# First bucket pass of a graph kernel: chunks in one stated order, equal source buckets counted on GpSimd

## The chip, the cores and the metric

The kernel runs on one core of a Trainium2 chip. Its engines have queues of their own and run side by side: TensorE (PE; its weight loads are listed as PEld), VectorE (DVE), ScalarE (ACT), GpSimd (POOL) and SyncE (SP), which here only issues transfers. The metric is the device time of one execution in microseconds (us), lower is better; the time given is the median of the runs.

## The reference

A graph of 10,000 nodes has 160,000 random edges (src, dst). Node features x (10,000 x 128) are passed along the edges seven times with a symmetric norm, and a small transformer block then reads the eight feature vectors of each node:

```
h = x; toks = [x]
for _ in range(7):
    msg = h[src] * deg_inv_sqrt[src, None] * deg_inv_sqrt[dst, None]
    h = segment_sum(msg, dst, N)
    toks.append(h)
tok = stack(toks, axis=1)                  # (N, 8, 128)
# layernorm, one attention block over the 8 tokens with wq, wk, wv, wo,
# then a softmax-weighted readout over the tokens with w_r -> (N, 128)
```

## The kernel before

The edges are sorted on the chip first, so that the seven hops can be done as products with 0/1 matrices. Destinations are cut into 79 buckets of 128 nodes, sources likewise into 72 buckets and a few cells. The change concerns the first bucket pass, which sorts the edges by destination bucket, and what stands around it. An edge sits at one of 128 partitions and 1250 columns; 50 columns make a chunk, 25 chunks in all.

**Preparing** (`pass_a`, lines 293 to 318). src and dst are loaded, and integer steps on DVE make `key` (the destination bucket), `d1` (src >> 3, plus 1) and `d2` (the other bits of src with the position of dst in its bucket). `first_rows` loads x on ACT's queue and scales its 79 tiles of 128 rows there. `lag` compares each column with the earlier ones of its chunk (49 comparisons on DVE, summed by PE into `wl`).

**The chunks** (lines 319 to 387). For each chunk: `oh` compares the keys with all 79 buckets (DVE, L226); `U` counts over the partitions (50 matmuls, L329), and ACT copies it to `U2`; `ux` multiplies it with `oh` (DVE, L239); `R` adds these up (17 matmuls, L243 and L244); `rk` reduces this to the rank of each edge in its bucket (DVE, L247). From the rank come one-hot rows over the 128 slots: `rv` for nine pairs of columns on DVE (L373) and `rs` for the other sixteen on ACT, one instruction per column (L360). `o` are the products of `oh` with `d1` and with `d2` (six instructions on DVE, L232). 50 matmuls (L385) add up `ta`, slot by bucket, in two halves, and `take` sums the halves on DVE into `TT` (L333), which then holds the packed edge of each slot. A scheduler sets the order of the instructions here from a loop that is already staggered: ranks of the next chunk and counts of the one after stand between the products of this one.

**The first table** (`first_table`, called at chunk 2). DVE takes the largest scaled entry of x (`mc`, L205), a few small steps make a power of two from it, and four times ACT writes 20 tiles as f16 (L177) while DVE writes what the rounding left (L178). Four transfers on SP's queue store the table.

**Decoding** (`decode`, lines 389 to 412). Once all of `TT` is there, nine passes over 128 x 2000 words get the source bucket `kB` and the 16-bit pattern `word` out of it on DVE and ACT; `lag_rows` compares `kB` with its earlier chunks (24 comparisons on DVE) and PE adds these up to `wB` (L285), the number of equal buckets ahead of each slot.

Then comes the second pass, interleaved with the first hop in an order written out by hand (`FRONT`), for which `pb_open` makes some constants. It reads `kB`, `wB`, `word` and `TT`. Six more hops and the attention follow. In the attention and the hops GpSimd has products (L1261, L1367), a scaling (L846) and a small copy (L737), and DVE small products (L1304, L1339) and a scaled subtraction (L838), by which the prediction prices and judges GpSimd's work.

Of the kernel before, what the change touches and what calls it, by code (L numbers as in the profile page):

```python
# [24 lines left out]
CELL = 334  # L25
CNODES = 196
# [32 lines left out]
2S1.2 0X1 3V1 1w0.2 2g2 3d1 3K3  # L59
"""  # L60


class Hops:
# [123 lines left out]
    def first_rows(self):  # L187
        nc, A = self.nc, self.nc.scalar
        tab0 = self.tab[0]
        y = self.tab[1].bitcast(F32)  # L190
        nc.gpsimd.memset(y[:, NT - 1:, :], 0.0)
        nc.gpsimd.memset(tab0[:, NT:, :], 0.0)
        h = NT // 2
        for a, b in ((0, h), (h, NT - 1)):
            nc.scalar.dma_start(y[:, a:b, :], self.x[a * 128:b * 128, :].rearrange("(t p) d -> p t d", p=128))
        nc.scalar.dma_start(y[:N - (NT - 1) * 128, NT - 1, :], self.x[(NT - 1) * 128:, :])
        for t in range(NT):
            A.activation(y[:, t, :], y[:, t, :], AF.Copy, scale=self.disT[:, t:t + 1])

    def first_table(self):  # L200
        nc, V = self.nc, self.nc.vector
        tab0, y = self.tab[0], self.tab[1].bitcast(F32)
        with self.tc.tile_pool(name="ft", bufs=1) as sp, self.tc.tile_pool(name="ftp", bufs=1, space=PSUM) as pp:
            mc = sp.tile([128, 1], F32, name="mc")
            V.tensor_reduce(mc, y[:, :NT, :], axis=mybir.AxisListType.XY, op=ALU.max, apply_absolute_value=True)  # L205
# [12 lines left out]
            q = self.pow2(pp, sp, m2, 2.0 ** 8)
            V.tensor_mul(self.sinv, self.sinv, q[:, 1:2])
            V.tensor_copy(self.q2, q[:, 0:1])  # L220


    def onehot(self, pool, name, key, n, size=None, **kw):
# [3 lines left out]
                                     self.io2[:, None, :n, :].to_broadcast([128, m, n, 2]), op=ALU.is_equal)  # L227
# [5 lines left out]

    def rank(self, wp, wu, R, oh, U2, w):

        nc, T = self.nc, self.nc.tensor
        m, nk, k = oh.shape[1], oh.shape[2], 5
        ux = wu.tile([128, m, nk, 2], F16, name="ux", tag="ux")
        nc.vector.tensor_tensor(ux, oh, U2[:, None].to_broadcast([128, m, nk, 2]), op=ALU.mult)  # L239
        R = R[:, :m * k * 2].rearrange("p (j k i) -> p j k i", k=k, i=2)  # L240
        for s in range(0, nk, k):
            e = min(k, nk - s)
            T.matmul(R[:, :, :e, :], self.id16, ux[:, :, s:s + e, :], start=s == 0, stop=False, skip_group_check=True)  # L243
        T.matmul(R[:, :, 0, :], self.id16, w, start=False, stop=True, skip_group_check=True)  # L244
        rk = wp.tile([128, m, 2], F16, name="rk")
        with nc.allow_low_precision("whole numbers; those over 2048 only have to stay large"):
            nc.vector.tensor_reduce(rk, R.rearrange("p j k i -> p j i k"), axis=X, op=ALU.add)  # L247
        return rk
# [21 lines left out]
    def lag_rows(self, ep, pp, key, w, m):  # L270

        V, T, k = self.nc.vector, self.nc.tensor, key.shape[2]
        n = 512 // k * k
        W = pp.tile([128, -(-m * k // n), 512], F32, name="W")
        flat = lambda z: z.rearrange("p m k -> p (m k)")
        parts = [(b, b * n, min(m * k, b * n + n)) for b in range(W.shape[1])]
        for b, r, e in parts:
            T.matmul(W[:, b, :e - r], self.id16, self.zero16[:, :e - r], start=True, stop=False, skip_group_check=True)
        for l in range(1, m):
            eq = ep.tile(list(key.shape), F16, name="eq")  # L280
            V.tensor_tensor(eq[:, l:], key[:, l:], key[:, :m - l], op=ALU.is_equal)
            for b, r, e in parts:
                r1 = max(r, l * k)
                if r1 < e:
                    T.matmul(W[:, b, r1 - r:e - r], self.id16, flat(eq)[:, r1:e], start=False, stop=(l + 1) * k >= e,  # L285
                             skip_group_check=True)
        for b, r, e in parts:
            self.nc.scalar.copy(flat(w)[:, r:e], W[:, b, :e - r])

    def pass_a(self):  # L290
        tc, nc, V, A, T, G = self.tc, self.nc, self.nc.vector, self.nc.scalar, self.nc.tensor, self.nc.gpsimd
        with ExitStack() as c:
# [5 lines left out]
            with tc.tile_pool(name="pe", bufs=1) as ep, tc.tile_pool(name="peq", bufs=3) as eqp, \  # L298
# [5 lines left out]
                it = ep.tile([128, 3, NCOL], I32, name="it")  # L304
                V.tensor_single_scalar(it[:, 0], ed[:, 1, :, 0], 7, op=ALU.arith_shift_right)
# [4 lines left out]
                V.tensor_tensor(it[:, 2], it[:, 2], it[:, 0], op=ALU.bitwise_or)  # L310
# [12 lines left out]

            def count(ch):
                oh = self.onehot(wp, "oh", K4[:, ch], NK)
                U = pp.tile([128, NK], F32, name="U")
                for j in range(NP):
                    for i in range(2):
                        T.matmul(U, self.tri, oh[:, j, :, i], start=j + i == 0, stop=j + i == NP)  # L329
                return oh, U  # L330

            def take(ch, ta):
                V.tensor_reduce(self.TT[:, ch, :NK], ta.rearrange("p h k -> p k h"), axis=X, op=ALU.add)  # L333

            def ranks(ch, oh, U):
                U2 = wp.tile([128, NK, 2], F16, name="U2")
                A.activation(U2, U[:, :, None].to_broadcast([128, NK, 2]), AF.Copy)
# [3 lines left out]
                A.activation(rb, rk[:, VP:], AF.Copy, scale=-2.0 ** 21, bias=16.0)
# [4 lines left out]
            cuts = (0, VP), (VP, VL), (VL, NP)
            ta = None
            for ch in range(NCH):
                if ch == 2:
                    self.first_table()  # L350
                oh, rk, rb = st
                ros = [wp.tile([128, b - a, 2, 128], F8, name=f"rs{a}") for a, b in cuts[1:]]
                for (a, b), ro in zip(cuts[1:], ros):
                    if ch == NCH - 1 and b == VL:
                        V.tensor_tensor(ro, rk[:, a:b, :, None].to_broadcast([128, b - a, 2, 128]),
                                        self.iof[:, None, None, :].to_broadcast([128, b - a, 2, 128]), op=ALU.is_equal, saturate=False)
                        continue
                    for j in range(a, b):
                        for i in range(2):
                            A.activation(ro[:, j - a, i, :], self.iof, AF.Abs_reciprocal_sqrt, scale=2.0 ** 21,  # L360
                                         bias=rb[:, j - VP, i:i + 1], saturate=False)
                o12 = [w1.tile([128, b - a, 2 * NK, 2], F16, name=f"o{a}") for a, b in cuts]

                def products(k):
                    a, b = cuts[k]
# [4 lines left out]
                if ch + 1 < NCH:  # L370
                    st = ranks(ch + 1, *nx)
# [1156 lines left out]
```

## Time and profile before

| | |
|---|---|
| runs | 3774.79, 3777.88, 3786.38 us (median 3777.88) |
| the profiled execution | 3821.03 us, its span 3819.1 us |
| granted TensorE clock, mean of the span | 0.976 |
| busy: PE, DVE, ACT, POOL | 94%, 79%, 72%, 44% |
| preparing and lags | up to 46.5 us |
| chunks and first table | up to 348.8 us |
| decoding | up to 378.3 us |

All times within a run are counted from the first instruction of the program. A line like L226 is a line of the kernel before; where a helper issues an operation, it is the helper's line. "out<-in" are the program's own names. "Busy" of an engine is the time in which at least one of its instructions ran; the mean of one instruction can be larger than busy time over count, since successive instructions overlap. Spans on POOL are rough. What ended an engine's idle time stands behind an arrow.

### The profile page before, as it was taken

The numbers are of one execution on the slowest core, as the hardware profiler recorded it, in microseconds if no ns is written. First come the engines' busy times: TensorE is split into PE (matmuls) and PEld (weight loads), VectorE is DVE, ScalarE is ACT, GpSimd is POOL, SyncE is SP. The second block draws the span as 40 slices with busy tenths as digits, with TensorE's granted clock in tenths as the row PEclk, the third lists the DMA queues.
The fourth block names the chain that finished last, engine by engine and source line by source line (L and its number), as shares of the span: only waits on it lengthen the run. The fifth ranks groups of instructions, "written<-read, shape, count | busy, mean of one in ns | idle before, by whom it ended". The sixth has DMA issues, their size and how long they took to land.

```text
span 3819.1 us, 173439 instructions
## 1 busy us (share of the span) xinstructions
PE 3594.5 (94%) x73707; PEld 2938.2 (77%) x73707; DVE 3019.8 (79%) x6994; ACT 2767.2 (72%) x6989; POOL 1681.5 (44%) x2230
## 2 busy tenths in 40 slices
PE   5887799999899999999999999999999998999997
PEld 4665678878688888887888788788878886777775
DVE  8998888888677777777777777777766665888888
ACT  6886488888766666766676666666756668888885
POOL 0000244444356656665666566566656661121111
PEclk8998899999999999999999999999999999999998
DMA  3100356556666666666666666666666552222220
GB/s 94 49 1 1 110 184 200 193 186 194 196 198 200 201 189 205 202 198 189 201 203 202 190 201 198 191 203 201 203 186 201 187 186 78 80 77 79 82 84 15
DMA packets 332728, 595.53 MB, mean 156 GB/s; under 512 B 57448, under 2 KB 225606, under 8 KB 326694
## 3 DMA queue, kind: packets, MB, share of 16 engines
q1 hardware_dynamic: 293989, 506.70, 42.5%
q0 software_dynamic: 35392, 72.55, 6.6%
q8 instruction: 577, 9.45, 1.0%
q10 hardware_dynamic: 2560, 5.12, 0.5%
q14 instruction: 210, 1.71, 0.2%
HBM read 455.49 MB, written 128.67 MB: 153 GB/s over the span
## 4 chain that ended last, share of the span: by engine, by line
PE 78%; DVE 9%; ACT 5%; DMA 4%; issue 3%; SPq 0%; POOL 0%; POOLq 0%; ACTq 0%; DVEq 0%
PE p L801 25%; PE acc L776 24%; PE acc L761 4%; PE pv L1172 4%; PE pu L1156 3%; PE p L667 3%; ACT rs L360 2%; PE po L1191 2%; PE pt L1146 2%; DVE o L232 2%; PE acc L654 2%; ACT eb L675 2%; PE acc L655 1%; PE ur L487 1%; PE ps L1221 1%
## 5 line engine op out<-in xcount | busy, mean ns | idle before, releaser
L806 ACT ACTIVATE eb<-p 128x512 f16<-128x512 f32 x2370 | 1258.3, 602 | 510.1 <-PE p L801 290.6
L808 DVE TENSOR_TENSOR eb<-p,eight 128x512 f16<-128x512 f32 x1896 | 1220.8, 686 | 328.3 <-PE acc L776 201.8
L801 PE MATMUL p<-tab,w 128*32 128x256 f16 x34128 | 1038.3, 274 | 20.1 <-issue 13.9
L776 PE MATMUL acc<-eb,w 128*128 128x256 f16 x8532 | 1011.7, 273 | 1.2 <-issue 1.2
L801 PEld LDWEIGHTS <-w 128*32 128x32 fp8e4 x34128 | 871.6, 97 | 161.9 <-issue 142.7
L776 PEld LDWEIGHTS <-w 128*128 128x128 fp8e4 x8532 | 835.5, 98 | 99.6 <-issue 2.0
L738 POOL DMA_INDIRECT og<-tabd,oidx x541 | 561.7, 1038 | 580.4 <-PE acc L776 286.6
L738 POOL DMA_INDIRECT og<-tabh,oidx x553 | 609.5, 1102 | 361.0 <-POOL og L737 121.9
L675 ACT ACTIVATE eb<-p 128x512 f16<-128x512 f32 x695 | 378.0, 626 | 30.6 <-PE p L667 24.8
L846 POOL TENSOR_SCALAR r<-s,ctok 128x128 f32<-128x128 f32 x474 | 293.5, 619 | 43.8 <-DVE s L792 26.4
L837 ACT ACTIVATE tab<-s,c 128x128 f16<-128x128 f32 x395 | 158.5, 401 | 200.9 <-DVE eb L808 172.3
L838 DVE SCALAR_TENSOR_TENSOR tab<-s,c,tab 128x128 f16<-128x128 f32 x395 | 138.9, 352 | 180.5 <-issue 169.3
L1261 POOL TENSOR_TENSOR p<-e,in 128x1024 f32<-128x1024 f32 (+1 forms) x40 | 76.5, 1913 | 446.5 <-DVE e L1260 446.5
L1213 ACT ACTIVATE junk<-tab 128x128 f32<-128x128 f32 x626 | 248.5, 401 | 8.3 <-SPq L1497 6.7
L667 PE MATMUL p<-tab,w 128*32 128x256 f16 x5688 | 210.7, 277 | 23.3 <-issue 12.4
L360 ACT ACTIVATE rs<-iof,rb 128x128 fp8e4<-128x128 f32 x784 | 231.8, 388 | 0.3
L792 DVE TENSOR_REDUCE s<-acc 128x128 f32<-128x256 f32 x474 | 196.9, 415 | 19.4 <-PE acc L790 11.7
L654 PE MATMUL acc<-eb,w 128*128 128x129 f16 x1422 | 203.4, 223 | 1.2 <-issue 0.4
L655 PE MATMUL acc<-eb,w 128*128 128x128 f16 x1422 | 201.5, 221 | 0.1
L737 POOL COPY og<-eb 128x1 f16<-128x1 f16 x452 | 83.1, 184 | 243.5 <-ACT eb L806 243.5
L667 PEld LDWEIGHTS <-w 128*32 128x32 fp8e4 x5688 | 137.8, 97 | 63.9 <-issue 41.4
L1172 PEld LDWEIGHTS pv<-Wv,xT 128*64 128x64 f32 x2504 | 138.9, 137 | 41.2 <-ACT uT L1157 29.3
(314 smaller groups left out, 5257.6 us busy)
## 6 DMA issues: line engine op xcount, KB each, us to landing
w<-gsd SPq DMA_DIRECT2D x474, 592.0 KB
gsd<-w SPq DMA_DIRECT2D x79, 592.0 KB
tok<-r SPq DMA_DIRECT2D x546, 64.0 KB
tab<-tok SPq DMA_DIRECT2D x273, 128.0 KB
rb<-srow SPq DMA_DIRECT2D x79, 352.0 KB
tabd<-tab SPq DMA_DIRECT2D x396, 64.0 KB
ra<-srow SPq DMA_DIRECT2D x79, 224.0 KB
og<-tabh,oidx POOLq DMA_INDIRECT x553
```

Of the source, the lines that this page charges most:

```text
L360: A.activation(ro[:, j - a, i, :], self.iof, AF.Abs_reciprocal_sqrt, scale=2.0 ** 21, bias=rb[:, j - VP, i:i + 1], saturate=False)
L654: T.matmul(acc[:, :129], W, rows[:, 128:257], start=start, stop=False, skip_group_check=True)
L667: T.matmul(p[32 * w:32 * w + 32, j], q["w", g][:, NJ * 128 + s * CAP:NJ * 128 + (s + 1) * CAP], tab[:, s, :], start=True, stop=True)
L675: A.activation(e[:, :, 0:256], pv, AF.Copy, scale=8.0)
L738: self.nc.gpsimd.indirect_dma_start(out=o, out_offset=None, in_=src[0] if i == NI else src[1], in_offset=bass.IndirectOffsetOnAxis(ap=self ...
L776: T.matmul(acc[0][:, :256], w[:, J * 128:(J + 1) * 128], e[:, j, :256], start=False, stop=J == NG - 1 and not late)
L801: T.matmul(p[32 * q:32 * q + 32, j], w[:, NJ * 128 + s * CAP:NJ * 128 + (s + 1) * CAP], tab[:, s, :], start=True, stop=True)
L806: A.activation(e[:, :n, 0:256], pv, AF.Copy, scale=8.0)
L808: V.tensor_tensor(e[:, :n, 0:256], pv, self.eight[:, :, None].to_broadcast([128, n, 256]), op=ALU.mult)
L846: self.nc.gpsimd.tensor_scalar(r, s, ct[:, t:t + 1], None, op0=ALU.mult)
L1172: T.matmul(p[64 * h:64 * h + 64, u - us[0], :], S[i]["xT"][:, h * m + q, 64 * c:64 * c + 64], Wv, start=True, stop=True, tile_position=(0, ...
L1213: A.activation(j, S[i]["x"][:, g, :], AF.Square, bias=S[i]["x"][:, g, 0:1], scale=-1.0, accum_out=R[i % 6][:, 0, g:g + 1])
```

## The change

- The integer steps ahead of the pass already make the source bucket (`d1`, with an offset) and the 16-bit pattern (`d2`, as the bits of an f16), so that the two products carry them as they are. That is three more one-input and three more two-input passes over 1250 columns.
- ACT copies both halves of `ta` to `KW` (`kw`); there is no `take` and no `decode`. Per chunk, `low` restores the packed edge in `TT` (one step on ACT, four on GpSimd over 80 columns), `eq` compares the chunk's buckets with those of all earlier chunks (GpSimd: a subtraction and a comparison with zero; DVE for the last chunk), and `W`/`wB` add these up (PE, ACT).
- ACT scales 56 of the 79 tiles ahead of the chunks, and the others four at a time within them. The largest entry is taken in eight parts; the table is written in eight parts, its subtraction on GpSimd in two steps instead of one on DVE. These steps run two per chunk from chunk 2 on.
- The order of every engine's instructions is stated: each word of `CHUNKS` is lateness, step and arguments, and the list is repeated for every chunk. `ux`, `eq` and two of the three `o` have one buffer, `rv` and the first `o` two.
- Constants and buffers of the next stage are made ahead of the pass; the second pass's one-hot counts from one.

```
+CHUNKS = """
+-1:U 0:rs:9:12 0:rv 0:rd 0:o:0 -1:U2 1:ta -1:ux 0:rs:12:17 1:kw 1:eq 1:low 0:Y 0:o:1 -1:R 0:rs:17:21 0:T 0:o:2 2:W 0:T 0:rs:21:25 2:wB -1:rk -1:rb -2:oh
+"""
...
+        for a, b in parts:
+            A.activation(tab0[:, a:b, 0:128], y[:, a:b, :], AF.Copy, scale=q[:, 0:1])
+            G.tensor_scalar(y[:, a:b, :], y[:, a:b, :], q[:, 0:1], None, op0=ALU.mult)
+            G.tensor_tensor(tab0[:, a:b, 128:256], y[:, a:b, :], tab0[:, a:b, 0:128], op=ALU.subtract)
+            yield
...
-                V.tensor_single_scalar(it[:, 1], ed[:, 0, :, 0], 3, op=ALU.arith_shift_right)
-                V.tensor_scalar(it[:, 2], ed[:, 0, :, 0], 7, 7, op0=ALU.bitwise_and, op1=ALU.logical_shift_left)
-                V.tensor_single_scalar(it[:, 0], ed[:, 1, :, 0], 127, op=ALU.bitwise_and)
-                V.tensor_tensor(it[:, 2], it[:, 2], it[:, 0], op=ALU.bitwise_or)
+                V.tensor_single_scalar(it[:, 1], sr, 7, op=ALU.arith_shift_right)
+                V.tensor_scalar(it[:, 1], it[:, 1], float(4 * NG), None, op0=ALU.min)
+                V.tensor_scalar(it[:, 2], sr, float(-n0), float(CELL), op0=ALU.add, op1=ALU.mult)
+                V.tensor_single_scalar(it[:, 2], it[:, 2], 16, op=ALU.arith_shift_right)
+                V.tensor_scalar(it[:, 2], it[:, 2], 0.0, None, op0=ALU.max)
+                V.tensor_scalar(it[:, 3], ds, 127, 1024, op0=ALU.bitwise_and, op1=ALU.bitwise_or)
+                V.scalar_tensor_tensor(it[:, 3], sr, 128.0, it[:, 3], op0=ALU.mult, op1=ALU.add)
+                V.scalar_tensor_tensor(it[:, 3], it[:, 1], -128.0 * 128, it[:, 3], op0=ALU.mult, op1=ALU.add)
+                V.scalar_tensor_tensor(w16, it[:, 2], -128.0 * CNODES, it[:, 3], op0=ALU.mult, op1=ALU.add)
+                V.tensor_tensor(it[:, 1], it[:, 1], it[:, 2], op=ALU.add)
...
+            def kw(ch, c):
+                A.copy(self.KW[:, :, ch, :NK], c["ta"])
+
+            def low(ch, c):
+                kB, TT = self.kB[:, ch], self.TT[:, ch]
+                A.activation(TT, self.word[:, ch].bitcast(I16), AF.Copy, bias=-17407.0)
+                t = [w1.tile([128, NTP], F32, name=f"tt{i}") for i in range(2)]
+                G.tensor_scalar(t[0], kB, float(4 * NG + 1), 128.0 * (CNODES - 128), op0=ALU.max, op1=ALU.mult)
+                G.tensor_scalar(t[1], kB, 128.0 * 128, -128.0 * (CNODES - 128) * (4 * NG + 1), op0=ALU.mult, op1=ALU.add)
+                for z in t:
+                    G.tensor_tensor(TT, TT, z, op=ALU.add)
+
+            def eq(ch, c):
+                if ch == 0:
+                    return
+                z = c["eq"] = w1.tile([128, last, NTP], F16, name="eqB")[:, :ch]
+                own = self.kB[:, ch, None, :].to_broadcast([128, ch, NTP])
+                if ch == last:
+                    V.tensor_tensor(z, self.kB[:, :ch], own, op=ALU.is_equal)
+                else:
+                    G.tensor_tensor(z, self.kB[:, :ch], own, op=ALU.subtract)
+                    G.tensor_scalar(z, z, 0.0, None, op0=ALU.is_equal)
+
+            def W(ch, c):
+                if ch:
+                    c["W"] = p1.tile([128, NTP], F32, name="WB")
+                    for k in range(ch):
+                        T.matmul(c["W"], self.id16, c["eq"][:, k], start=k == 0, stop=k == ch - 1)
+
+            def wB(ch, c):
+                if ch:
+                    A.copy(self.wB[:, ch], c["W"])
...
+                for it in range(-2, NCH + 4):
+                    for word in CHUNKS.split():
+                        late, z, *a = word.replace(":", " ").split()
+                        if z == "T":
+                            if it >= 2:
+                                next(more, None)
+                        elif z == "Y":
+                            if it >= 0:
+                                self.scale_rows(rest[:4])
+                                del rest[:4]
+                        elif 0 <= it - int(late) < NCH and (z != "rd" or it - int(late) == last):
+                            F[z](it - int(late), C[it - int(late)], *(int(k) for k in a))
...
             self.pass_a()
-            self.decode()
```

The other steps of the chunks (`oh`, `U`, `U2`, `ux`, `R`, `rk`, `rb`, `rv`, `rs`, `o`, `ta`) issue the instructions that stood in the loop before.

More of the change, by code (lines that the diff above doesn't have):

```diff
@@ L223, in onehot, with scale_rows, pow2_steps @@
-    def onehot(self, pool, name, key, n, size=None, **kw):
+    def scale_rows(self, ts):
+        y = self.tab[1].bitcast(F32)
+        for t in ts:
+            self.nc.scalar.activation(y[:, t, :], y[:, t, :], AF.Copy, scale=self.disT[:, t:t + 1])
+    def pow2_steps(self, pp, sp, col, cap):
+        V, T = self.nc.vector, self.nc.tensor
+        pm = pp.tile([128, 512], F32, name="pm", tag="acc")[0:1, 0:128]
+        T.transpose(pm, col, self.ident)
+        yield
+        r = sp.tile([1, 1], F32, name="r11")
+        V.tensor_reduce(r, pm, axis=X, op=ALU.max)
+        V.tensor_scalar(r, r, 1e-30, 1.0 / BIG, op0=ALU.max, op1=ALU.mult)
+        V.reciprocal(r, r)
+        V.tensor_scalar(r, r, cap, None, op0=ALU.min)
+        V.tensor_single_scalar(r.bitcast(I32), r.bitcast(I32), 0x7F800000, op=ALU.bitwise_and)
+        pb = pp.tile([128, 512], F32, name="pb", tag="acc")[:, 0:1]
+        T.matmul(pb, self.ones32, r, start=True, stop=True)
+        yield
+        q = sp.tile([128, 2], F32, name="q2")
+        V.tensor_copy(q[:, 0:1], pb)
+        V.tensor_scalar(q[:, 1:2].bitcast(I32), q[:, 0:1].bitcast(I32), -1.0, float(254 << 23), op0=ALU.mult, op1=ALU.add)
+        return q
@@ L224, in onehot @@
+    def onehot(self, pool, name, key, n, size=None, base=0, **kw):
         m = key.shape[1]
@@ L232, in times @@
         self.nc.vector.tensor_tensor(out, oh, f[:, :, None, :].to_broadcast(list(oh.shape)), op=ALU.mult)
[L234 to L248, printed above, removed]
     def zeros(self, ep):
@@ L268, in lag @@
             self.nc.scalar.copy(w[:, r:e, :], out(b, e - r))
[L270 to L288, printed above, removed]
     def pass_a(self):
@@ L327, in count, with oh, U @@
+            C = [dict() for _ in range(NCH)]
+            def oh(ch, c):
+                c["oh"] = self.onehot(wp, "oh", K4[:, ch], NK)
+            def U(ch, c):
+                c["U"] = pp.tile([128, NK], F32, name="U")
                 for j in range(NP):
                     for i in range(2):
[L329 to L333, printed above, removed]
@@ L346, in pass_a @@
[L346 to L356, printed above, removed]
-                        continue
[L358 to L365, printed above, removed]
-                    self.times(o12[k][:, :, :NK], oh[:, a:b], D1[:, ch, a:b])
-                    self.times(o12[k][:, :, NK:], oh[:, a:b], D2[:, ch, a:b])
-                products(0)
-                if ch + 1 < NCH:
-                    st = ranks(ch + 1, *nx)
-                rv = w1.tile([128, VP, 128, 2], F16, name="rv")
-                V.tensor_tensor(rv, rk[:, :VP, None, :].to_broadcast([128, VP, 128, 2]),
-                                self.io2[:, None].to_broadcast([128, VP, 128, 2]), op=ALU.is_equal)
-                products(1)
-                products(2)
-                if ch + 2 < NCH:
-                    nx = count(ch + 2)
-                if ch:
-                    take(ch - 1, ta)
-                ta = pp.tile([128, 2, NK], F32, name="ta")
@@ new lines, in R @@
+            def R(ch, c):
+                k = 5
+                c["R"] = pp.tile([128, 512], F32, name="R")[:, :NP * k * 2].rearrange("p (j k i) -> p j k i", k=k, i=2)
+                for s in range(0, NK, k):
+                    e = min(k, NK - s)
+                    T.matmul(c["R"][:, :, :e, :], self.id16, c["ux"][:, :, s:s + e, :], start=s == 0, stop=False, skip_group_check=True)
+                T.matmul(c["R"][:, :, 0, :], self.id16, W4[:, ch], start=False, stop=True, skip_group_check=True)
@@ new lines, in rk, with rb @@
+            def rk(ch, c):
+                c["rk"] = wp.tile([128, NP, 2], F16, name="rk")
+                with nc.allow_low_precision("whole numbers; those over 2048 only have to stay large"):
+                    V.tensor_reduce(c["rk"], c["R"].rearrange("p j k i -> p j i k"), axis=X, op=ALU.add)
+            def rb(ch, c):
+                c["rb"] = wp.tile([128, NP - VP, 2], F32, name="rb")
+                A.activation(c["rb"], c["rk"][:, VP:], AF.Copy, scale=-2.0 ** 21, bias=16.0)
+                c["ro"] = [None] + [wp.tile([128, b - a, 2, 128], F8, name=f"rs{a}") for a, b in cuts[1:]]
@@ new lines, in rs, with o @@
+            def rs(ch, c, a, b):
+                for j in range(a, b):
+                    k = 1 if j < VL else 2
+                    if k == 1 and ch == last:
+                        continue
+                    for i in range(2):
+                        A.activation(c["ro"][k][:, j - cuts[k][0], i, :], self.iof, AF.Abs_reciprocal_sqrt, scale=2.0 ** 21,
+                                     bias=c["rb"][:, j - VP, i:i + 1], saturate=False)
+            def o(ch, c, k):
+                a, b = cuts[k]
+                z = c["o", k] = (w1 if k else wp).tile([128, b - a, 2 * NK, 2], F16, name=f"o{a}")
+                self.times(z[:, :, :NK], c["oh"][:, a:b], D1[:, ch, a:b])
+                self.times(z[:, :, NK:], c["oh"][:, a:b], D2[:, ch, a:b])
@@ new lines, in pass_a @@
+            with tc.manual_schedule():
+                more = self.first_table(sp, fp)
+                rest = list(range(ROWS, NT))
+                for it in range(-2, NCH + 4):
[10 more added lines that the diff above has]
+                            F[z](it - int(late), C[it - int(late)], *(int(k) for k in a))
+                for _ in more:
+                    pass
@@ L855, in run @@
             G.memset(self.TT[:, :, NK:], 0.0)
+            self.KW = self.bp.tile([128, 2, NCH, NTP], F16, name="KW")
+            self.kB, self.word = self.KW[:, 0], self.KW[:, 1]
+            self.wB = self.bp.tile([128, NCH, NTP], F16, name="wB")
+            G.memset(self.KW[:, :, :, NK:], 0.0)
+            G.memset(self.wB[:, 0], 0.0)
+            base, self.ebuf = self.ebuf, []
+            self.more_ebufs(self.bp, 8 - len(base))
+            self.extra, self.ebuf = self.ebuf, base
+            self.og1 = [[self.bp.tile([128, 260], F16, name=f"og{j}{b}") for b in range(2)] for j in range(NI + 1)]
+            for o in (o for z in self.og1 for o in z):
+                G.memset(o, 1.0)
+            with tc.tile_pool(name="pbc", bufs=1) as tp:
+                self.pb_constants(tp)
             self.pass_a()
-            self.decode()
             self.gsp = c.enter_context(tc.tile_pool(name="gs1", bufs=6))
```

146 lines of the change are left out of this document (68 added, 78 removed).

## Prediction

> **What bounds the kernel now.** I read the page first, then the busy time by stage, then the chain that ended last, then the groups of instructions inside the stage that the change rewrites. The page's first part, and three stages of the span (columns: window, its length, then busy us and instruction count of PE, PEld, DVE, ACT, POOL, then PE clock, DMA share, GB/s):
>
> ```profile
> PE 3594.5 (94%) x73707; PEld 2938.2 (77%) x73707; DVE 3019.8 (79%) x6994; ACT 2767.2 (72%) x6989; POOL 1681.5 (44%) x2230
> ...
> 0.00:46.50 46.50, 22.92 (x151) 13.85 (x152) 39.21 (x102) 28.80 (x92) 7.61 (x30) 0.92 0.54 167
> 46.50:348.80 302.30, 244.61 (x2931) 197.56 (x2930) 284.45 (x293) 251.13 (x844) 0.00 (x0) 0.90 0.07 20
> 348.80:378.30 29.50, 16.52 (x85) 8.47 (x85) 27.95 (x35) 3.65 (x3) 1.08 (x4) 0.71 0.00 1
> ```
>
> The whole is bound by PE in the hops, but the change touches only the first 378 us: loading and lag counting (to 46.5), the 25 chunks with the first table (to 348.8), the decoding (to 378.3). There DVE is the fullest engine (284 of 302 us) and POOL does nothing. The chain confirms it (start us, us, what):
>
> ```profile
> 46.54 10.69 DVE mc L205
> ...
> 343.22 5.00 PE ta L385 x50
> ...
> 364.50 13.75 PE W L285 x75
> 378.27 2.15 DVE oh L226
> ```
>
> From 378.27 on the next stage runs as before, so the end of this stretch is what moves. The groups of the middle window (xcount | busy us, mean ns of one | idle before):
>
> ```profile
> L360 ACT ACTIVATE rs<-iof,rb 128x128 fp8e4<-128x128 f32 x784 | 231.8, 388 | 0.3
> L232 DVE TENSOR_TENSOR o<-oh,d 128x1264 f16<-128x1264 f16 x96 | 74.0, 812 | 3.0 <-PE ta L385 2.7
> L239 DVE TENSOR_TENSOR ux<-oh,U 128x3950 f16<-128x3950 f16 x25 | 55.2, 2210 | 0.4 <-ACT U L337 0.4
> L226 DVE TENSOR_TENSOR oh<-key,io 128x3950 f16<-128x3950 f16 x23 | 50.8, 2208 | 0.0
> L232 DVE TENSOR_TENSOR o<-oh,d 128x1422 f16<-128x1422 f16 x48 | 40.9, 893 | 4.5 <-PE ta L385 4.5
> L373 DVE TENSOR_TENSOR rv<-rk,io 128x2304 f16<-128x2304 f16 x25 | 33.8, 1351 | 0.0
> L247 DVE TENSOR_REDUCE rk<-R 128x50 f16<-128x250 f32 x25 | 10.4, 417 | 7.2 <-PE R L244 7.1
> L178 DVE SCALAR_TENSOR_TENSOR tab<-tab,q,tab 128x2560 f16<-128x2560 f32 x3 | 8.5, 2867 | 0.0
> L333 DVE TENSOR_REDUCE TT<-ta 128x79 f32<-128x158 f32 x25 | 7.9, 317 | 2.7 <-PE ta L385 2.7
> L177 ACT ACTIVATE tab<-tab,q 128x2560 f16<-128x2560 f32 x3 | 7.1, 2412 | 0.0
> L337 ACT ACTIVATE U<-U 128x158 f16<-128x158 f32 x25 | 6.9, 286 | 9.9 <-PE U L329 6.3 <-issue 3.6
> L341 ACT ACTIVATE rb<-rk 128x32 f32<-128x32 f16 x25 | 5.5, 218 | 37.4 <-DVE rk L247 37.4
> ```
>
> The first table costs DVE about 24 us in there: mc 10.7, four subtractions 11.3 (8.5 for three and a fourth taken alike), some 2 us of small steps. What is left of 284.45 is 260.5 us for 24.2 chunks (two of 25 one-hots and one of 25 product sets ran before the window), so 10.8 us of DVE per chunk; the stage itself took (302.3 - 24) / 24.2 = 11.5 per chunk. ACT has 231.8 / 25 = 9.3 plus 0.29 plus 0.22.
>
> **The period after the change.** DVE loses the reduce of L333, and is left with about 10.45 us per chunk. But the stated order closes a ring through PE: one-hot of chunk n+2 (last on DVE), counts U, then the products ta of the chunk before and the ranks R, which sit between in PE's queue, then rk, then the next one-hot. PE's pieces where they ran without waiting:
>
> ```profile
> 232.57 2.04 PE L243 MATMUL R<-ux,id 128*128 128x250 f16 x16 [1.21 <-DVE ux L239]
> 234.44 0.19 PE L244 MATMUL R<-wl,id 128*128 128x50 f16 x1
> 234.47 2.08 PE L385 MATMUL ta<-o,rs 128*128 128x158 f16 x23
> 237.26 2.10 PE L329 MATMUL U<-oh,tri 128*128 128x79 f16 x50 [0.71 <-DVE oh L226]
> 240.38 1.49 PE L385 MATMUL ta<-o,rv 128*128 128x158 f16 x18 [0.37 <-DVE rv L373]
> ```
>
> The ring: U 2.10, ta 1.49 + 32/23 of 2.08 = 4.38, R 2.04 + 0.19, rk 0.42, one-hot 2.21, together 11.3, with hand-overs about 11.4 us. So the period is 11.4 and not 10.45, and DVE has 1.0 us of slack in it. The new matmuls that add equal buckets (W, up to 24 of 80 columns, about 1 us at U's rate) lie beside rk and the one-hot. ACT gets a copy, a conversion and a wB copy, about 0.25 to 0.3 each by L337: 10.6, under the period.
>
> **Ahead of the chunks.** Preparing the edges gets three more one-input passes and three more two-input ones over 1250 columns, 2.4 + 4.3 = 6.8 us of DVE by these rows:
>
> ```profile
> L305 DVE TENSOR_SCALAR it<-ed x1: 814/814/814, 6.4 to 6.4; 128x1250 int32<-128x1250 int32 x1
> ...
> L310 DVE TENSOR_TENSOR it<-it 128x1250 int32<-128x1250 int32 x1 | 1.4, 1444 | 0.0
> ...
> L198 ACT ACTIVATE tab<-tab,disT x79: 386/391/402, 23.3 to 46.1; 128x128 f32<-128x128 f32 x79
> ```
>
> Against that, the two one-hots and the product set that ran there (about 9 us) move behind it, and ACT scales 56 of the 79 rows there (0.29 us each from first to last, done at about 40). So the chunks begin at 46.5 - 9 + 6.8 = 44.3. The constants of the next stage only change places.
>
> **Sum without GpSimd.** Begin 44.3; filling the pipeline (one-hot 2.2, U 2.1, copy 0.3, ux 2.2, R 2.2, rk 0.4, one-hot 2.2) 11.6; 25 periods of 11.4 are 285. The first table rides along: mc in eight parts, 10.7 us of DVE over four iterations with 1.0 of slack each, +7; the other 23 rows on ACT, 1.2 us against 0.8 of slack in six iterations, +2; the table's copies on ACT (four of 2.4 in 9.5 us), 2.4 against 0.8 in four iterations, +6. Its DMAs leave SP's queue one every half chunk; nothing else stands there, and the hops read the table much later. Behind the last chunk: ta 4.4, copy 0.3, one comparison on DVE 1.1, W about 1.4, copy 0.3, 7.5. Together 363.4, with the decoding's 29.5 us gone from the path: **15 us** before the 378.3 of now. With the 11.5 of now as the period it is 12; with DVE's own 10.45, 39, and no more.
>
> **What GpSimd costs.** It gets, per chunk c, one subtraction and one comparison of 80c elements (c = 1 to 23, together 22,080), two scalings and two additions of 80, and for the table eight scalings and eight subtractions of 1280. Prices of its instructions:
>
> ```profile
> L1261 POOL TENSOR_TENSOR p<-e,in 128x1024 f32<-128x1024 f32 x39 | 76.1, 1951 | 433.9 <-DVE e L1260 433.9
> L1367 POOL TENSOR_TENSOR Ab<-sel,rz 128x128 f32<-128x128 f32 x78 | 30.1, 406 | 73.7 <-DVE rv L1300 58.6 <-PE pu L1156 9.8 <-DVE rv L1306 4.2
> L846 POOL TENSOR_SCALAR r<-s,ctok 128x128 f32<-128x128 f32 x474 | 293.5, 619 | 43.8 <-DVE s L792 26.4 <-issue 0.4
> L737 POOL COPY og<-eb 128x1 f16<-128x1 f16 x452 | 83.1, 184 | 243.5 <-ACT eb L806 243.5
> ```
>
> Two inputs: (1951 - 406) / 896 = 1.72 ns per element and 0.19 us at the start. So the subtractions cost 22,080 x 1.72 ns + 23 x 0.19 = 42.3 us, the small additions 50 x 0.32 = 16.2, the table's 8 x 2.39 = 19.1: **77.6 us**. One input: 81 instructions of at least 0.4 (between 184 and 619 ns), at most 0.62 each with 1.72 ns for every element over 128; that is 33 to 98, I take 65, near L846's 81 x 0.62 = 50. In sum some 143 us in a stretch of 320, so GpSimd can keep up if it runs beside DVE. Does it? Here it is off duty in this stretch, so I looked for places where both work on SBUF (start us, us; minimum/median/maximum ns):
>
> ```profile
> 3206.44 1.95 POOL L1261 TENSOR_TENSOR p<-e,in 128x1024 f32<-128x1024 f32 x1 [14.21 <-DVE e L1260]
> ...
> 3207.05 1.39 DVE L1304 TENSOR_TENSOR rx<-v 128x16 f32<-128x16 f32 x1
> ...
> L1304 DVE TENSOR_TENSOR rx<-v x40: 150/182/1386, 3179.9 to 3774.4; 128x16 f32<-128x16 f32 x39, 128x2 f32<-128x2 f32 x1
> ...
> 3812.42 0.77 POOL L1367 TENSOR_TENSOR Ab<-sel,rz 128x128 f32<-128x128 f32 x2 [4.17 <-DVE rv L1306]
> ...
> 3812.89 0.34 DVE L1339 TENSOR_TENSOR rz<-ry 128x32 f32<-128x32 f32 x1 [0.56 <-ACT ry L1314]
> ...
> L1339 DVE TENSOR_TENSOR rz<-ry x46: 191/193/336, 3178.6 to 3815.7; 128x32 f32<-128x32 f32 x46
> ...
> 2002.03 0.62 POOL L846 TENSOR_SCALAR r<-s,ctok 128x128 f32<-128x128 f32 x1
> ...
> 2002.23 0.35 DVE L838 SCALAR_TENSOR_TENSOR tab<-s,c,tab 128x128 f16<-128x128 f32 x1 [0.47 <-issue]
> ```
>
> L1304 needs 0.18 us and took 1.39 the one time that it met L1261: it ended at 3208.44, 0.05 behind GpSimd's 3208.39. L1339 needs 0.19, took 0.34 and ended at 3813.23, 0.04 behind GpSimd's 3813.19. So a DVE instruction with two inputs from SBUF is held until a two-input GpSimd instruction is over. The last pair shows no such hold beside a one-input GpSimd instruction: L838 lies inside L846 and neither is longer than elsewhere. In the chunks all of DVE but rk has two inputs from SBUF (oh, ux, rv, o), so every two-input GpSimd instruction there stops DVE for its length. Of 77.6 us the ring's slack of 1.0 us takes about half where it can, 12 us of a possible 25; some 65 reach the path. 65 - 15 is **+50**: bounds +38 (all the slack used) to +63 (none), if one-input instructions hold nothing.
>
> The Trainium skill (SBUF — State Buffer, "Who interferes with whom") speaks against the change more strongly: a DVE instruction with two SBUF inputs contends with any GpSimd instruction that reads SBUF, and whichever comes second is fully blocked. The trace agrees for L1304 and L1339, and not for L838.
>
> **Rivals.** (a) One-input GpSimd instructions hold DVE too, since L846 reads only 128 elements and may have read them in the 0.20 us before L838 began: nearly all of the 65 us comes on top, some 55 with DVE's rk and waits taken off, so +105, 3883. This is the page's rule taken whole. (b) Faster: the hold seen with f32 operands does not bite with f16, or GpSimd finds its time in DVE's waits. Then the sum without GpSimd stands, -15, 3763; for it speaks only that the rows which show a hold are two and short. It decides when less than 15 of the 77.6 us reach the path. (c) The holds just eat the gain, within 0.3% (11 us, about what a measurement here can tell from no change): 4 to 26 us reach the path. (d) The counting does not run beside the chunks as stated: DVE's instructions follow each other closely, GpSimd gets in only at rk and a wait, about two turns a chunk for its three two-input instructions. W stands in PE's queue ahead of the next U and waits for it, one ring in two is a half longer: 25 x 0.5 x 11.4 = 142, less 15 is +127, 3905.
>
> **How the numbers follow.** The profiled run took 3821.03 us, span 3819.1 and 1.9 around it; the runs' median is 43 lower, 1.1%, and 1.1% of +50 is 0.6, so I take the difference from the median as it is: 3777.9 + 50 = 3828. Chances: the forecast 0.36, (a) 0.17, (d) 0.04, (b) 0.33 of which 0.02 ends within 0.3%, (c) 0.10. That is faster 0.31, same 0.12, slower 0.57. The likeliest case's own range is 3816 to 3841. Both signs hold much, so the range reaches from a good case of (b), -24, 3754, to (a), 3883; beyond it lie (d), the upper half of (a) and the best of (b), together under 0.2.
>
> **What would show it.** In the changed profile: no int32 decoding and no 13.75 us of W; the period by two ux of successive chunks, 11.4 early and, if the forecast holds, 10.45 + 0.84 + 0.14c us late (14 at c = 20), since the hold shows as DVE's oh, ux, rv and o lasting longer than 2.21, 2.21, 1.35 and 0.8; an unchanged median of these with GpSimd busy beside them is (b). Longer DVE instructions under the comparison of GpSimd as well are (a). PE waiting at W for GpSimd is (d). Wrong it would be if DVE's groups keep their means, or if the stages after the chunks change.

## The result and the profile after

The changed kernel takes 3871.91 us, median of four runs (3862.51 to 3881.31), against 3780.65 us for the kernel before on the same chip (four runs, 3774.79 to 3786.38). The ratio is 1.0241, with a 95% interval of 1.021 to 1.0273: 91 us slower. The profiled execution of the changed kernel took 3881.31 us, the longest of its four, its span 3879.5. The page's first part:

```profile
PE 3571.1 (92%) x73922; PEld 2970.1 (77%) x73922; DVE 3099.4 (80%) x6946; ACT 2735.2 (71%) x7060; POOL 1978.7 (51%) x2394
```

DVE has 48 instructions fewer than before (6946 against 6994) and is busy 80 us longer (3099.4 against 3019.8). That is the sign to follow: fewer instructions that last longer. The busy time by stage (columns as in the prediction; one-hots of keys begin at 45.9, and the second pass's first one-hot, which stood at 378.3, now begins at 469.4):

```profile
0.00:45.90 45.90, 23.41 (x151) 14.01 (x151) 38.44 (x99) 22.34 (x69) 10.26 (x36) 1.00 0.55 169
45.90:469.40 423.50, 256.62 (x3231) 238.86 (x3231) 391.97 (x281) 278.47 (x943) 302.28 (x162) 0.77 0.05 15
...
230.00:330.00 100.00, 56.53 (x674) 52.10 (x674) 91.61 (x66) 59.25 (x201) 94.55 (x46) 0.73 0.16 44
```

The stretch ends 469.4 - 378.3 = 91.1 us later, and the medians differ by 91.3, so the loss lies here. The two profiles alone don't show that the stages behind it are as they were: the profiled execution of the kernel before (3821.03 us) is as long as those on the second chip below, and what follows its 378.3 took 3440.8 us, against 3410.1 behind 469.4. But in the experiments below, on both chips, end and median move together within 6 us. Where the table is made (230 to 330) even GpSimd, at 94.55 of 100 us, is the fullest engine. The groups of the stretch from 45.9 to 469.4 (lines are those of the changed kernel; xcount | busy us, mean ns of one | idle before):

```profile
L269 DVE TENSOR_TENSOR o<-oh,d 128x1422 f16<-128x1422 f16 (+1 forms) x150 | 158.9, 1109 | 2.6 <-PE ta L403 2.6
L427 POOL TENSOR_SCALAR eqB<-eqB 128x80 f16<-128x80 f16 (+22 forms) x23 | 86.5, 3760 | 2.0
L263 DVE TENSOR_TENSOR oh<-key,io 128x3950 f16<-128x3950 f16 x25 | 80.1, 3206 | 0.4 <-PE W L287 0.4
L375 DVE TENSOR_TENSOR rv<-rk,io 128x2304 f16<-128x2304 f16 x25 | 67.5, 2699 | 0.0
L353 DVE TENSOR_TENSOR ux<-oh,U 128x3950 f16<-128x3950 f16 x25 | 62.7, 2507 | 16.4 <-ACT U L349 16.3
L416 POOL TENSOR_TENSOR TT<-TT,tt 128x80 f32<-128x80 f32 x50 | 56.9, 1138 | 4.0
L426 POOL TENSOR_TENSOR eqB<-KW 128x80 f16<-128x80 f16 (+22 forms) x23 | 55.4, 2410 | 76.5 <-ACT rs L389 43.3 <-PE WB L433 25.9 <-ACT KW L407 7.2
L249 POOL TENSOR_SCALAR tab<-tab,q 128x1280 f32<-128x1280 f32 (+1 forms) x8 | 37.1, 4634 | 0.0
L250 POOL TENSOR_TENSOR tab<-tab,tab 128x1280 f16<-128x1280 f32 (+1 forms) x8 | 26.3, 3286 | 0.7
L413 POOL TENSOR_SCALAR tt<-KW 128x80 f32<-128x80 f16 x25 | 23.9, 955 | 61.3 <-ACT KW L407 59.4
L414 POOL TENSOR_SCALAR tt<-KW 128x80 f32<-128x80 f16 x25 | 16.6, 664 | 2.0
L366 DVE TENSOR_REDUCE rk<-R 128x50 f16<-128x250 f32 x25 | 10.2, 407 | 3.9 <-PE R L361 3.8
```

The four DVE groups with two inputs from SBUF have grown: one-hot 2.208 to 3.206 us, ux 2.210 to 2.507, rv 1.351 to 2.699, o 0.839 (96 at 812 ns and 48 at 893) to 1.109. Times their counts that is 25.0 + 7.4 + 33.7 + 40.5 = 106.6 us. The one that reads PSUM has not: rk 417 before, 407 after.

How it happens shows in one chunk period late in the stretch. DVE (start us, us), and then GpSimd's counting of equal buckets in the same time:

```profile
402.57 2.36 DVE L353 TENSOR_TENSOR ux<-oh,U 128x3950 f16<-128x3950 f16 x1
404.86 3.15 DVE L269 TENSOR_TENSOR o<-oh,d 128x1264 f16<-128x1264 f16 x4
407.93 0.41 DVE L366 TENSOR_REDUCE rk<-R 128x50 f16<-128x250 f32 x1
408.26 4.91 DVE L263 TENSOR_TENSOR oh<-key,io 128x3950 f16<-128x3950 f16 x1
413.08 4.41 DVE L375 TENSOR_TENSOR rv<-rk,io 128x2304 f16<-128x2304 f16 x1
417.42 1.80 DVE L269 TENSOR_TENSOR o<-oh,d 128x1422 f16<-128x1422 f16 x2
419.15 2.36 DVE L353 TENSOR_TENSOR ux<-oh,U 128x3950 f16<-128x3950 f16 x1
```
```profile
407.89 3.20 POOL L426 TENSOR_TENSOR eqB<-KW 128x1600 f16<-128x1600 f16 x1 [2.73 <-PE WB L433]
411.18 6.09 POOL L427 TENSOR_SCALAR eqB<-eqB 128x1600 f16<-128x1600 f16 x1
```

From ux to ux it is 16.58 us, and DVE has no gap in it. The one-hot lasts 4.91 us, 2.7 over its own time: it ends at 413.17, which is 2.08 us, about its own 2.21, behind the end of the subtraction at 411.09. Then the two change places. The comparison L427 starts at 411.18 but gets nowhere until the one-hot is over at 413.17; rv starts at 413.08 and ends at 417.49, so its own 1.35 us began at 416.14. That is 1.1 us **before** the comparison's recorded end at 417.27, and 2.97 us behind the one-hot's end, 1.86 ns for each of the comparison's 1600 elements. So the one-input comparison holds DVE as well, though not to its end: I read this as until its input is read, the rest being writing; that reason is not shown, and spans on GpSimd are rough.

### The profile page after: what moved, and what is told of

It reads as the page before. It is cut to its first block, busy times and chain, and to the rows that moved or that the text cites. A ratio compares the mean times of both kernels' runs of the same rounds, so it can differ in the third digit from the quotient of the medians.

```text
span 3879.5 us, 174108 instructions
## 1 busy us (share of the span) xinstructions
PE 3571.1 (92%) x73922; PEld 2970.1 (77%) x73922; DVE 3099.4 (80%) x6946; ACT 2735.2 (71%) x7060; POOL 1978.7 (51%) x2394
## 5 line engine op out<-in xcount | busy, mean ns | idle before, releaser
L852 ACT ACTIVATE eb<-p 128x512 f16<-128x512 f32 x2370 | 1212.6, 609 | 522.9 <-PE p L847 522.9
L854 DVE TENSOR_TENSOR eb<-p,eight 128x512 f16<-128x512 f32 x1896 | 1180.0, 683 | 297.7 <-PE p L847 295.5
L847 PE MATMUL p<-tab,w 128*32 128x256 f16 x34128 | 1024.9, 274 | 5.0 <-DVE same L1131 4.6
L784 POOL DMA_INDIRECT og<-tabh,oidx x553 | 601.3, 1087 | 338.8 <-POOL og L783 122.3
L721 ACT ACTIVATE eb<-p 128x512 f16<-128x512 f32 x695 | 374.6, 622 | 19.2 <-PE p L713 15.6
L884 DVE SCALAR_TENSOR_TENSOR tab<-s,c,tab 128x128 f16<-128x128 f32 x395 | 168.5, 427 | 180.5 <-ACT tab L883 180.5
L713 PE MATMUL p<-tab,w 128*32 128x256 f16 x5688 | 205.8, 279 | 25.1 <-ACT eb L721 16.6
L838 DVE TENSOR_REDUCE s<-acc 128x128 f32<-128x256 f32 x474 | 196.6, 415 | 18.0 <-PE acc L836 14.6
L345 PE MATMUL U<-oh,tri 128*128 128x79 f16 x1250 | 82.4, 257 | 107.6 <-DVE oh L263 107.6
```

Of the source, the lines that this page charges most:

```text
L713: T.matmul(p[32 * w:32 * w + 32, j], q["w", g][:, NJ * 128 + s * CAP:NJ * 128 + (s + 1) * CAP], tab[:, s, :], start=True, stop=True)
L721: A.activation(e[:, :, 0:256], pv, AF.Copy, scale=8.0)
L784: self.nc.gpsimd.indirect_dma_start(out=o, out_offset=None, in_=src[0] if i == NI else src[1], in_offset=bass.IndirectOffsetOnAxis(ap=self ...
L847: T.matmul(p[32 * q:32 * q + 32, j], w[:, NJ * 128 + s * CAP:NJ * 128 + (s + 1) * CAP], tab[:, s, :], start=True, stop=True)
L852: A.activation(e[:, :n, 0:256], pv, AF.Copy, scale=8.0)
L854: V.tensor_tensor(e[:, :n, 0:256], pv, self.eight[:, :, None].to_broadcast([128, n, 256]), op=ALU.mult)
```

## The experiments

Two theories on why the stretch grew by 91 us when the prediction had +50. **Two inputs only** (the forecast): just the subtractions and additions hold DVE, and the rest of the loss is late chunks and waits. **Any reading** (rival a): every GpSimd instruction that reads SBUF holds it. Kernels of one table were timed against the same runs of the kernel before. "End" is where the second pass's first one-hot begins; 378.3 before, 469.4 after. e2, e3 and e7 have two runs each, the others 8 to 12.

| | median, us | ratio to before (95%) | end, us |
|---|---|---|---|
| kernel before, first chip | 3779.89 | | |
| e1_no_gpsimd | 3784.79 | 1.0007 (0.9997 to 1.0018) | 381.7 |
| e2_one_input | 3846.00 | 1.0169 (1.0142 to 1.0197) | 448.5 |
| e3_two_inputs | 3828.14 | 1.0122 (1.0095 to 1.015) | 432.1 |
| e4_write_only | 3787.68 | 1.0016 (1.0003 to 1.0029) | 383.2 |

**e1_no_gpsimd** is the changed kernel with GpSimd's work given to DVE: the counting in one comparison per chunk, placed at the end of the list; the table's remainder in one step, one part late; the packed edge restored in three passes behind the second pass's first step.

```
-... 1:kw 1:eq 1:low ... -2:oh
+... 1:kw 1:low ... -2:oh 1:eq
-            G.tensor_scalar(y[:, a:b, :], y[:, a:b, :], q[:, 0:1], None, op0=ALU.mult)
-            G.tensor_tensor(tab0[:, a:b, 128:256], y[:, a:b, :], tab0[:, a:b, 0:128], op=ALU.subtract)
+                a, b = parts[i - 1]
+                V.scalar_tensor_tensor(tab0[:, a:b, 128:256], y[:, a:b, :], q[:, 0:1], tab0[:, a:b, 0:128], op0=ALU.mult, op1=ALU.subtract)
-                    G.tensor_tensor(z, self.kB[:, :ch], own, op=ALU.subtract)
-                    G.tensor_scalar(z, z, 0.0, None, op0=ALU.is_equal)
+                V.tensor_tensor(z, self.kB[:, :ch], own, op=ALU.is_equal)
```

> The changed kernel with everything that it gave to GpSimd taken by DVE: the comparison with earlier chunks as one instruction at the end of each chunk's list (about 0.16 + 0.04c us), the table's subtraction in one step one part late, and the packed edges restored in three passes behind the first one-hot of the next stage. Theory H (GpSimd's reads of SBUF hold DVE's instructions with two SBUF inputs, and that is the whole loss): oh, ux, rv and o are back at 2.21, 2.21, 1.35 and 0.81 to 0.89 us, a chunk takes 11.4 to 11.8, and the stretch ends near 375 us (363 without GpSimd, some 10 of DVE's new work) instead of 469; total near 3777, between 3765 and 3795. Rival O (the stated order itself, its ring through PE or the single buffers, is what lost the time): a chunk still takes 14 us or more, the stretch ends past 430, total above 3830.

Measured: 3784.79 us, no difference from the kernel before, end at 381.7. Its groups between 45 and 452 us:

```profile
L265 DVE TENSOR_TENSOR oh<-key,io 128x3950 f16<-128x3950 f16 x25 | 55.1, 2206 | 0.4 <-PE W L289 0.4
L377 DVE TENSOR_TENSOR rv<-rk,io 128x2304 f16<-128x2304 f16 x25 | 33.8, 1351 | 0.0
L420 DVE TENSOR_TENSOR eqB<-KW 128x80 f16<-128x80 f16 (+23 forms) x24 | 16.1, 672 | 2.5 <-PE WB L426 2.5
L252 DVE SCALAR_TENSOR_TENSOR tab<-tab,q,tab 128x1280 f16<-128x1280 f32 (+1 forms) x8 | 12.3, 1532 | 5.1 <-ACT tab L249 5.1
```

With GpSimd idle, one-hot and rv are back at 2.21 and 1.35 us. So GpSimd's work in the chunks costs 469.4 - 381.7 = 87.7 us more than the same work on DVE. (The restoring of the packed edge lies behind e1's end; the medians, which have it in, differ by 87.1.) And DVE does the counting of 24 chunks in 16.1 us, where GpSimd needs 55.4 + 86.5 for 23 of them, its waits for a turn included.

The end still came some 7 us later than the 375 I had in mind. Two views of this kernel say why: the stages (first two lines), and the waits of DVE between 80 and 240 us (engine, line, releaser: us in total, times, longest).

```profile
85.00:240.00 155.00, 101.11 (x1293) 95.40 (x1291) 137.81 (x144) 126.65 (x418) 0.00 (x0) 0.81 0.10 27
240.00:370.00 130.00, 100.54 (x1515) 94.23 (x1516) 128.24 (x136) 118.25 (x419) 0.00 (x0) 0.95 0.05 15
```
```profile
DVE ux L355 <- ACT U L351: 8.0, 10, 1.5
DVE tab L252 <- ACT tab L249: 5.1, 4, 2.4
DVE o L271 <- PE ta L405: 3.9, 6, 1.1
```

While the table rides along DVE is idle 155.0 - 137.8 = 17.2 us, and the three waits make 17.0 of it. The first belongs to a ring that the prediction did not count: one-hot, counts U, copy, ux. Behind the table (240 to 370) DVE is full, and from 259 us on the chunks take 11.0 to 11.8 us.

**e2_one_input, e3_two_inputs, e4_write_only** are e1 with one GpSimd instruction more per chunk, behind a one-element copy that sets when it may start; nobody reads its result. In e2 and e3 it has 1536 elements, where the counting has 80 to 1840; the memset of e4 has 3840 and so lasts about as long.

```
+                G.tensor_copy(scr[:, 0, 0:1], self.KW[:, 0, ch, 0:1])
+                G.tensor_scalar(scr[:, :6], con, 0.0, None, op0=ALU.is_equal)        # e2
+                G.tensor_tensor(scr[:, :6], con, con, op=ALU.subtract)               # e3
+                G.memset(scr[:, :15], 0.0)                                           # e4
```

> e1 with idle work added on GpSimd in chunks 1 to 24: a copy of one element that follows the chunk's buckets, then one comparison with a constant over 1536 elements of a constant (one SBUF input), into a tile that nobody reads. Nothing waits for it. Theory H for all reads: DVE is held while the instruction reads, about 1536 x 1.85 ns = 2.8 us in each chunk, less up to 1 us of slack: the stretch grows by 45 to 70 us over e1. Rival T (only GpSimd instructions with two inputs hold, as the prediction took it): within 8 us of e1, and DVE's means unchanged. The instruction itself should take about 0.3 + 1536 x 2.5 ns = 4.1 us where it isn't held.

> e1 with, in place of e2's comparison, a subtraction of the constant from itself over 1536 elements (two SBUF inputs), 0.19 + 1536 x 1.72 ns = 2.8 us. Theory H and rival T alike: held for its length, the stretch grows by 45 to 70 us over e1. Rival O: no one waits for it, so nothing.

> e1 with, in place of e2's comparison, a memset of 3840 elements (no input, some 4 us). Theory H (the reads hold): within 8 us of e1, DVE's means unchanged. Rival P (any long GpSimd instruction beside DVE's two-input instructions holds them): the stretch grows by 60 to 95 us.

Measured against e1's end: +66.8 us for the one-input comparison, +50.4 for the subtraction, +1.5 for the writing. The two groups that matter in each, between 45 and 452 us; e2:

```profile
L421 POOL TENSOR_SCALAR Sov<-io 128x1536 f16<-128x1536 f16 x24 | 107.2, 4467 | 2.0
L265 DVE TENSOR_TENSOR oh<-key,io 128x3950 f16<-128x3950 f16 x25 | 80.6, 3225 | 0.4 <-PE W L289 0.4
```

e3:

```profile
L421 POOL TENSOR_TENSOR Sov<-io 128x1536 f16<-128x1536 f16 x24 | 73.8, 3075 | 1.9
L265 DVE TENSOR_TENSOR oh<-key,io 128x3950 f16<-128x3950 f16 x25 | 76.1, 3042 | 0.4 <-PE W L289 0.4
```

e4:

```profile
L421 POOL MEMSET Sov<- 128x3840 f16 x24 | 79.1, 3297 | 1.4
L265 DVE TENSOR_TENSOR oh<-key,io 128x3950 f16<-128x3950 f16 x25 | 55.1, 2206 | 0.4 <-PE W L289 0.4
```

The e4 instruction lasts longer than that of e3 and leaves the one-hot at 2.206 us. So it is the reading that holds, with one input as with two, and the theory of two inputs only falls. The one-input instruction is even the dearer: for the same 1536 elements it took 4.47 us against 3.08, and 66.8 / 24 = 2.8 us of it reached the path against 2.1. When e2's hold ends, its trace shows (GpSimd, then DVE):

```profile
307.96 4.54 POOL L421 TENSOR_SCALAR Sov<-io 128x1536 f16<-128x1536 f16 x1
```
```profile
308.61 0.42 DVE L368 TENSOR_REDUCE rk<-R 128x50 f16<-128x250 f32 x1
308.94 4.75 DVE L265 TENSOR_TENSOR oh<-key,io 128x3950 f16<-128x3950 f16 x1
```

The reduction from PSUM runs inside GpSimd's instruction at its usual length. The one-hot ends at 313.69, so its own 2.21 us began at 311.48, 1.0 us before GpSimd's 312.50. In all ten chunks of e2 in which the comparison meets the one-hot this distance is 1.02 us; beside the subtraction of e3 it is 0.13 to 0.15.

A second group ran on another chip, on which the kernel before takes longer, so only ratios and ends are compared with the first:

| | median, us | ratio to before (95%) | end, us |
|---|---|---|---|
| kernel before, second chip | 3816.84 | | |
| e5_swap | 3813.95 | 1.000 (0.999 to 1.0009) | 373.5 |
| e6_swap_late | 3809.81 | 0.998 (0.9971 to 0.9989) | 367.4 |
| e7_equal_only | 3880.25 | 1.017 (1.0152 to 1.0188) | 443.2 |

**e5_swap** is e1 with the next one-hot ahead of the reduction of ranks, so that the counts U and their copy start sooner.

```
-... 2:wB -1:rk -1:rb -2:oh 1:eq
+... 2:wB -2:oh -1:rk -1:rb 1:eq
```

> e1 with the next one-hot moved ahead of rk in the stated order (DVE: o, oh, rk, eq instead of o, rk, oh, eq), so that DVE no longer waits for R before it and U has time to run beside rk, eq, rv and o. In e1 ux waited 8.0 us for U2 in ten chunks from 85 to 240 us, where U2 came 3.6 us behind the one-hot, and a chunk took 14 to 16 us there and 11.1 to 11.8 late. Theory R (the ring through U, ta, R, rk and oh adds to DVE's own time): a chunk takes 10.9 to 11.2 late and 12.5 to 14 early; the stretch ends 10 to 25 us before e1's 381.7; total 3755 to 3772, ratio near 0.996. Rival D (DVE's own instructions set the time, the waits are only where the slack shows): within 5 us of e1.

Measured: the end 8.2 us earlier than e1's, less than the least that I expected, and no difference from the kernel before in the whole. The wait of ux was real, but between 80 and 240 us it only fell from 8.0 to 4.2 us, and that of the products for ta from 3.9 to 1.7: 6.0 of the 8.2 us.

**e6_swap_late** lets the table's remainder follow one part later still, so that DVE no longer waits for ACT's half.

```
-        for i, (a, b) in enumerate([*parts, (0, 0)]):
+        for i, (a, b) in enumerate([*parts, (0, 0), (0, 0)]):
-            if i:
-                a, b = parts[i - 1]
+            if i > 1:
+                a, b = parts[i - 2]
```

> e5 with the table's subtraction one more part later, so that DVE does not wait for ACT's copy of the same step (in e1 5.1 us in four waits, the longest 2.4). Expected 4 to 7 us under e5 if those waits lie on the path, the same as e5 if ACT is the bound in those chunks.

Measured: 6.1 us more off the end, and with 0.998 the one version that beats the kernel before, by 7 us. Its stages:

```profile
85.00:240.00 155.00, 104.63 (x1385) 97.82 (x1382) 147.75 (x159) 134.77 (x445) 0.00 (x0) 0.86 0.14 38
240.00:360.00 120.00, 93.18 (x1418) 87.18 (x1419) 119.37 (x122) 110.56 (x391) 0.00 (x0) 0.95 0.01 2
```

DVE is busy 147.75 of 155 us with the table and 119.37 of 120 behind it: there is little left to win by order; from here it is DVE's own time that counts.

**e7_equal_only** is e1 with only the counting back on GpSimd, at the place that the change gave it; table and packed edge stay on DVE.

```
-... 1:kw 1:low ... -2:oh 1:eq
+... 1:kw 1:eq 1:low ... -2:oh
-                V.tensor_tensor(z, self.kB[:, :ch], own, op=ALU.is_equal)
+                if ch == last:
+                    V.tensor_tensor(z, self.kB[:, :ch], own, op=ALU.is_equal)
+                else:
+                    G.tensor_tensor(z, self.kB[:, :ch], own, op=ALU.subtract)
+                    G.tensor_scalar(z, z, 0.0, None, op0=ALU.is_equal)
```

> The changed kernel with only the counting of equal buckets left on GpSimd (subtraction and comparison of 80c elements, c = 1 to 23, where the changed kernel has them); table and packed edges on DVE as in e1. Theory H, all reads hold: subtractions 42 us, comparisons 22,080 x 1.85 ns = 41 us of reading, 83 in sum less up to 15 of slack, so 55 to 80 us over e1's 381.7. If the two-input ones alone held: 30 to 42 over e1. The rest of the 88 us between e1 and the changed kernel then belongs to table and packed edges.

Measured: the end at 443.2, 61.5 us behind e1's, as expected if every reading holds and more than the two-input instructions alone would give. So the counting alone makes 61.5 of the 87.7 us between e1 and the changed kernel. The other 26.2 belong to the table and the packed edge. By the starts of successive ux the changed kernel is 1.3 us ahead of e7 at 187.32, 21.4 behind it at 291.90 and 24.5 behind at 386.24. The table's steps run on GpSimd from 187.57 to 281.5, so most of the 26.2 comes with them, and the packed edge, which goes on all along, adds little: 3.1 us from 291.90 to 386.24. How the table costs, the changed kernel shows between 242 and 259 us, GpSimd first, then DVE, then the waits of the whole stretch:

```profile
242.64 4.17 POOL L249 TENSOR_SCALAR tab<-tab,q 128x1280 f32<-128x1280 f32 x1
246.89 4.01 POOL L250 TENSOR_TENSOR tab<-tab,tab 128x1280 f16<-128x1280 f32 x1
250.88 4.72 POOL L249 TENSOR_SCALAR tab<-tab,q 128x1280 f32<-128x1280 f32 x1
255.68 2.60 POOL L250 TENSOR_TENSOR tab<-tab,tab 128x1280 f16<-128x1280 f32 x1
```
```profile
248.35 10.61 DVE L269 TENSOR_TENSOR o<-oh,d 128x1264 f16<-128x1264 f16 x4
```
```profile
PE WB L433 <- POOL eqB L427: 31.7, 4, 14.0
```

Four products that need 3.2 us together (4 at 812 ns) last 10.61: the shortest took 0.80 us, the longest 3.60, with a wait for a turn in it. And the counting queued behind the table on GpSimd is late, so that PE stands at W. Of the two the first sets the time: in the whole stretch DVE is busy 391.97 us, against 360.36 in e7 (45.7 to 443.2), and idle 31.5 against 37.1.

## Why the prediction was right in kind and short in size

**The hold: right.** The forecast's mechanism was that GpSimd stops DVE where both read SBUF, and the two short meetings it was read from (L1304, L1339) meant what they seemed to. Rival (b), no hold with f16, is refuted by e2 and e3 against e1; rival (c) by the 91 us.

**The step that failed: "if one-input instructions hold nothing".** I took that from L838 inside L846, which reads only 128 elements. At the 1.86 ns an element of the reading above, those are read in 0.24 us, and L838 began 0.20 us in: the pair could not show a hold. Rival (a) said exactly this and gave +105; measured is +91. The median, 3871.91, lies well beyond the forecast's own 3816 to 3841; it is within the range as a whole because that reached as far as (a). The Trainium skill (SBUF — State Buffer, "Who interferes with whom") has it that a DVE instruction with two SBUF inputs contends with a GpSimd instruction that reads SBUF, not with one that only writes it. The runs agree on both: e2 +66.8 us and e3 +50.4, e4 +1.5. On the length of the block, which the page gives as the whole instruction, the subtraction of e3 agrees within 0.15 us, but the one-input instructions let DVE go 1.0 to 1.1 us before their recorded end.

**Terms of the sum.** Two-input instructions: I let 65 of 77.6 us reach the path. The price was right (0.19 + 1536 x 1.72 ns = 2.83 us; the shortest in e3 took 2.745), the share was not: at that price e3's 24 cost 67.9 us, of which 50.4 reached the path, 0.74, and of 77.6 that leaves 58. Two of the small additions of `low` took 0.79 us at the least, where I had 0.64. One-input instructions: priced at 65 us in all and put at nothing on the path. They lasted 86.5 + 23.9 + 16.6 + 37.1 = 164 us with their waits for a turn, and the comparison's recorded length grows from 5.09 us at 1200 elements to 6.09 at 1600, 2.5 ns an element, not the 1.72 that I had as the most. With 58 for the first kind and the forecast's gain of 15, which no run shows by itself, 91 leaves 48 for the second. This split is worked out, not measured: the two kinds take turns on the same DVE instructions.

**Without GpSimd: 363.4.** No run shows this kernel without GpSimd's work. e1 has it on DVE, where it costs 16.1 + 12.3 us, and ends at 381.7, so between 353.3 and 381.7 would be left without it; the change as it stands, less the 106.6 us by which DVE's instructions grew, gives 469.4 - 106.6 = 362.8. 363.4 agrees with both, but neither is a measurement of it, and the parts were off: the chunks begin at 45.9 and not 44.3; with the table riding along most periods of e1 took 13.5 to 16.4 us, where I had 11.4 and 15 us on top in all; and the ring had a wait in it that I had not seen, of ux for the copy of U (8.0 us in that stretch of e1, 16.3 in all of the changed kernel). The 11.4 itself can't be told from DVE's own time: the last periods of e6 are 11.2 to 11.4 us, and DVE's own are 10.45 and nearly one of comparisons.

**Period and rival (d).** At chunk 20 I expected 14 us; it is 16.58, with DVE full. The counting did come late, by 31.7 us in four waits of PE at W, but not by one ring in two: three of them (25.8 us) came while the table stood ahead of it on GpSimd, the fourth (5.9) in the last chunks. And DVE's idle time is no longer than in e7 (31.5 us against 37.1), so (d) is not the cause. What stays open: how the 26.2 us divide exactly between table and packed edge, and whether the swap of e5 would help the changed kernel, whose ux waits 16.3 us for the copy of U. Neither was tried.

## What to carry to other kernels

Before work is moved to an idle GpSimd, look at what DVE runs at that time: if it has two inputs from SBUF and no slack, GpSimd instructions that read SBUF, those with one input too, are paid for on DVE's path, here 2.1 to 2.8 us for 1536 elements that DVE compares in some 0.9 us itself. Two kinds of pairs ran freely here: a memset on GpSimd beside DVE's two-input instructions (e4), and DVE's reduction from PSUM beside a comparison on GpSimd (e2). When a short pair in a trace is to show that something does *not* collide, work out first whether it lasted long enough to collide.

## What the runs showed of the hardware that I had not expected

- On GpSimd the one-input comparison of 1536 f16 elements took 4.47 us on the mean and the two-input subtraction 3.08; the shortest took 4.08 and 2.745.
- The two engines took turns instruction by instruction here, whoever waited going next. In the period shown, subtraction, one-hot, comparison and rv ran strictly one after the other, and each carries its wait in its recorded time; the subtraction's is the least, 3.20 us where the price gives 2.94.
- DVE's reduction `mc`, with one input from SBUF, kept its 1.48 us in e2 the four times that it ran beside the comparison, and the comparison its 4.08 to 4.11.
- PE's clock was lower where DVE was held and PE waited; why, no run shows. The mean matmul of U took 212 ns before (granted clock 0.90 in its stretch), 237 in e1 (0.86) and 257 after (0.77).
